# 128-column weights issued as two 64-column halves, with written orders of issue, in a four-layer spectral and state-space kernel

## The chip, the cores and the metric

The kernel runs on one core of a Trainium2 chip. The metric is the device time of one execution in microseconds (us). TensorE is called PE here (its weight loads PEld), VectorE DVE, ScalarE ACT, GpSimd POOL, and SyncE SP.

## What is computed

The input is one sequence of 2048 rows with 512 channels. Four layers follow one another, A, B, A, B, each with a layer norm ahead of it and a residual around it:

```python
def _A_ref(x, w_r, w_i):
    X = rfft2(x, axes=(-2, -1)); X = X * (w_r + 1j * w_i)
    return irfft2(X, s=(S, D), axes=(-2, -1))
def _B_ref(u, log_A_real, A_imag, C_real, C_imag, log_dt, D_skip):
    dt = exp(log_dt); A = -exp(log_A_real) + 1j * A_imag
    C = (C_real + 1j * C_imag) * dt[:, None]
    K = 2.0 * einsum("dn,dnl->dl", C, exp((A * dt[:, None])[:, :, None] * pos)).real
    y = irfft(rfft(u_t, 2 * L) * rfft(K, 2 * L))[:, :, :L]
    return y + u * D_skip
x = A_x
x = x + _A_ref(_layernorm(x), w_r, w_i);  x = x + _B_ref(_layernorm(x), ...)
x = x + _A_ref(_layernorm(x), w_r, w_i);  x = x + _B_ref(_layernorm(x), ...)
```

A is a two-dimensional Fourier transform, a product with fixed weights, and the transform back. B is a convolution along the rows with a kernel K for each of the 512 channels, made from 128 decaying oscillations a channel; both B layers use the same K.

## The kernel before

All transforms are matrix products with constant matrices, in two factors (2048 = 16 x 128 for A, 4096 = 32 x 64 x 2 for B), in f32, which PE does in two passes. Every layer runs in steps, and a step is a Python function that issues a few matmuls and what takes their results out of PSUM.

Layer A (`layer_a`): `spread` (in the second layer A `spread_four`) normalizes the rows and does the first factor along the rows, four products of 128 columns of weights by 128 of data for each of 16 groups (L462, L492). `middle` runs over 16 groups of frequencies: `forward` does the transform along the channels (L503 to L507) and copies it out as `z` on ACT (L517), `weigh` does the second factor in pairs through `side_by_side` (L322) and multiplies by the weights on DVE (L533) and adds on DVE and POOL (L538), `back` returns along the second factor (L551). `end` goes back along the channels (`fold`, L580 to L583) and the rows (`rows_back`, L601).

The convolution kernel K (`kernel_parts`, `kernel_time`): `kernel_parts` prepares phases and logarithms, mostly on DVE, and writes them in three bf16 parts to memory. `kernel_time` then makes K in 32 units of two halves: `grow` (matmul L847, ACT exponential), `bend` (matmuls L857 and L858 in bf16, rounding `kw` on DVE at L860, matmul L861 that subtracts it), `sine` and `cosine` on ACT into a tile `qp` (L826), `terms` on DVE (L879, L881), and `total` (matmul L892, 64 columns of weights, alternating between the two column halves of the array). `kernel_freq` transforms K, 128 channels at a time, and keeps it in memory.

Layer B (`layer_b`): for each of four blocks of 128 channels, `rows` (64*64 tiles: four quarters of the array at once), a transpose of 32x32 squares on DVE (L660), `pair` (64-column weights, `side_by_side`), products with K on DVE (L984), sums on POOL and DVE (L996), `units` (one 128-column product L1004 and 64 small ones of 64 columns, copied out by ACT at L1009), and `rows` again with the residual (L1023).

`side_by_side` at L322 issues products that lie on different parts of the array, so that they run at the same time. Where a product has 128 columns of weights it is one matmul.

The order of work before: the streams of steps are interleaved in Python (`interleave`), and a scheduler then orders the instructions of each engine, with hints at a few places (`issue_after` and a high priority, in `side_by_side`, `ordered`, `spread_four`, `units` and `fetch`). Tiles of a pool take turns in a fixed number of buffers ("rooms"), and which tile gets which follows from the schedule too.

## Time and profile before

| What | Value |
|---|---|
| runs (median, lowest, highest of 3) | 778.15, 777.2, 783.55 us |
| profiled execution, and its span | 785.32 us, 783.6 us |
| mean granted clock of PE | 0.922 |
| PE busy, matmuls | 81%, 7248 |
| DVE busy, instructions | 82%, 1283 |
| ACT busy, instructions | 55%, 928 |
| POOL busy, instructions | 53%, 596 |

How to read the rows: a line such as L462 is a line of the kernel before; `p<-w,w` is the tile that is written and those that are read, without numbers; `128*64` is a matmul's rows and columns of weights, and what follows is the data that it streams. "f32 x96" is a count. The time of a matmul ends when its results are out, so matmuls that follow one another overlap, and the distance of two starts tells what one costs. In the waits, a line names who waited, for whom, how long in all, how often, and the longest.

### The profile page before, as it was taken

How to read it: one execution, taken by the hardware profiler on the slowest of the kernel's cores; microseconds unless marked ns; L12 is line 12 of the kernel's file. 1: busy time of each engine (PE TensorE's matmuls, PEld its weight loads, DVE VectorE, ACT ScalarE, POOL GpSimd, SP SyncE). 2: the span in 40 equal slices, each digit the busy share in tenths (PEclk: the TensorE clock that was granted, in tenths of full speed). 3: DMA queues.
4: the chain of work that ended last, by engine and by line, in shares of the span. 5: the costliest groups of instructions: out<-in, count | busy, mean ns of one | idle time of the engine just before them, and what ended most of it. 6: DMA issues, size and time to landing. Idle time of an engine off the chain costs nothing. (4 is left out here: it accounts for less than half of the span.)

```text
span 783.6 us, 18760 instructions
## 1 busy us (share of the span) xinstructions
PE 631.2 (81%) x7248; PEld 445.6 (57%) x7248; DVE 642.5 (82%) x1283; ACT 431.3 (55%) x928; POOL 414.0 (53%) x596
## 2 busy tenths in 40 slices
PE   3038799898877986897789887874999897889986
PEld 2037576666544544565365647654877664457666
DVE  5998589698988879868997996778588597788993
ACT  3425997875545875787578725223766335233322
POOL 4587766838350454911675573371055473376850
PEclk9995899999967999999999998877999898799999
DMA  8400452324517542361335449122122104124413
GB/s 286 178 0 21 147 180 63 54 83 103 175 49 170 165 87 64 98 171 44 62 110 129 150 73 280 71 95 68 55 81 82 28 16 147 55 83 137 128 38 109
DMA packets 137337, 81.01 MB, mean 103 GB/s; under 512 B 70977, under 2 KB 116929, under 8 KB 136353
## 3 DMA queue, kind: packets, MB, share of 16 engines
q1 hardware_dynamic: 136992, 79.30, 35.8%
q8 instruction: 57, 0.93, 0.5%
q0 software_dynamic: 256, 0.52, 0.4%
q14 instruction: 32, 0.25, 0.1%
HBM read 54.90 MB, written 25.43 MB: 103 GB/s over the span
## 5 line engine op out<-in xcount | busy, mean ns | idle before, releaser
L996 POOL TENSOR_TENSOR u<-wb,wb 64x512 f32<-64x512 f32 x90 | 128.4, 1427 | 90.4 <-DVE wb L984 75.1
L322 PE MATMUL p<-z,mb 128*64 128x512 f32 (+1 forms) x480 | 104.6, 545 | 9.1 <-DVE wb L984 5.9
L892 PE MATMUL pv<-qp 128*64 128x128 f32 x1024 | 79.9, 300 | 11.6 <-DVE qp L881 6.4
L984 DVE TENSOR_TENSOR wb<-p,kk 128x512 f32<-128x512 f32 x128 | 80.8, 675 | 6.4 <-PE p L322 5.2
L892 PEld LDWEIGHTS pv<-qp 128*64 128x64 f32 x1024 | 63.4, 150 | 39.5 <-ACT stage L900 12.8
L654 ACT COPY z<-p 128x512 f32<-128x512 f32 x96 | 51.5, 599 | 57.5 <-PE p L322 44.3
L322 PE MATMUL p<-mb,u 128*64 128x64 f32 x2048 | 73.4, 236 | 11.4 <-DVE u L996 4.2
L322 PEld LDWEIGHTS p<-mb,u 128*64 128x64 f32 x2048 | 71.2, 151 | 19.7 <-issue 11.6
L881 DVE TENSOR_TENSOR qp<-qp,mag 128x1024 f32<-128x1024 f32 x64 | 81.7, 1282 | 0.9
L1108 POOL TENSOR_SCALAR w<-w,norms 128x128 f32<-128x128 f32 x64 | 51.2, 811 | 52.6 <-DMA w<-h 35.4
L879 DVE SCALAR_TENSOR_TENSOR qp<-qp,mag 128x256 f32<-128x256 f32 x128 | 66.5, 536 | 12.6 <-ACT qp L826 12.0
L660 DVE STREAM_TRANSPOSE z<-z 128x512 f32<-128x512 f32 x96 | 58.5, 674 | 20.4 <-ACT z L654 20.4
L462 PE MATMUL p<-w,w 128*128 128x128 f32 x128 | 30.3, 414 | 46.1 <-DVE w L455 35.4
L533 DVE TENSOR_TENSOR w<-wt,p 128x514 f32<-128x514 f32 x64 | 42.5, 686 | 29.5 <-PE p L322 24.1
L538 POOL TENSOR_TENSOR w<-w,w 64x257 f32<-64x257 f32 x48 | 36.6, 762 | 53.5 <-DVE w L533 48.2
L1009 ACT COPY u<-p 128x512 f32<-128x512 f32 x64 | 37.7, 590 | 47.4 <-PE p L322 45.4
L322 PEld LDWEIGHTS p<-z,mb 128*64 128x64 f32 x480 | 35.3, 144 | 39.6 <-issue 20.9
L462 PEld LDWEIGHTS p<-w,w 128*128 128x128 f32 x128 | 26.4, 303 | 49.7 <-issue 31.9
L826 ACT ACTIVATE kf<-pk 128x512 f32<-128x512 f32 x64 | 38.9, 608 | 24.3 <-PE pk L861 23.8
L592 POOL TENSOR_TENSOR wv<-w 128x254 f32<-128x254 f32 x32 | 26.6, 831 | 45.0 <-DVE w L589 33.2
L551 PE MATMUL p<-ca,w 128*128 128x128 f32 x256 | 40.8, 290 | 8.6 <-POOL w L540 3.9
L322 PE MATMUL p<-t,w 64*64 64x128 f32 x1024 | 43.3, 289 | 5.3 <-issue 2.8
(189 smaller groups left out, 1528.2 us busy)
## 6 DMA issues: line engine op xcount, KB each, us to landing
wt<-in_w SPq DMA_DIRECT2D x32, 257.0 KB
kf<-kk SPq DMA_DIRECT2D x32, 256.0 KB
kk<-kf SPq DMA_DIRECT2D x32, 256.0 KB
u<-in_x SPq DMA_DIRECT2D x16, 256.0 KB
hr<-in_x SPq DMA_DIRECT2D x16, 256.0 KB
kt<-stage SPq DMA_DIRECT2D x32, 128.0 KB
h<-hr SPq DMA_DIRECT2D x16, 256.0 KB
w<-kt SPq DMA_DIRECT2D x32, 128.0 KB
```

The source lines that it names most:

```text
L322: last = self.nc.tensor.matmul(out, weights, data, start=not more, stop=True, skip_group_check=True).ins
L462: nc.tensor.matmul(p[:, b], xf[:, b], t, start=True, stop=True)
L533: nc.vector.tensor_mul(m[pl], W, px[:, None, :].to_broadcast([128, 2, 257]))
L551: nc.tensor.matmul(p[:, oe, v], Y[:, v, 128 * oe:128 * oe + 128], st, start=True, stop=True, skip_group_check=True)
L654: nc.scalar.copy(tiles["z"][:, :, :, b, m:m + 2].rearrange("p u j m r -> p (u j) (m r)"), ps[b].rearrange("p u j m r -> p (u j) (m r)"))
L660: nc.vector.transpose(tiles["zt"][:, u:u + 8].rearrange("p u j d -> p (u j d)"), tiles["z"][:, u:u + 8].rearrange("p u j b m r -> p (u j b ...
L879: nc.vector.scalar_tensor_tensor(QP[:, c, 0], QP[:, c, 1, :, ::-1], -1.0 if c else 1.0, m[:, 0], op0=ALU.mult, op1=ALU.mult)
L881: nc.vector.tensor_mul(t, t, mag[:, None, 1:3, 256 * j:256 * j + 256].to_broadcast([128, 2, 2, 256]))
L892: nc.tensor.matmul(p[64 * t:64 * t + 64, g], QP[:, c, 2, d:d + 2].rearrange("p s a -> p (s a)"), QP[:, c, 0:2, d:d + 2].rearrange("p k s b ...
L984: nc.vector.tensor_mul(split(m[c, pl], "du", [32, 16]), by_channel(p), split(k[c], "du", [32, 16]))
L996: self.added = e[0].tensor_sub(y[0:64], v[0, 0], v[1, 1]), e[1].tensor_add(y[64:128], v[0, 1], v[1, 0])
L1108: (self.nc.gpsimd if XNE[k] == "g" else self.nc.vector).tensor_scalar(t[:, k], t[:, k], scale, bias, op0=ALU.mult, op1=ALU.add)
```

## The change

Two things change. First, a helper `halves` issues each matmul with 128 columns of weights as two with 64 columns, to the lower and the upper half of the output's partitions. It replaces every such matmul: L462, L492, L503 to L507, L551, L580 to L583, L601, L847, L857, L858, L861 and L1004. The data streamed is the same, once for each half.

Second, the hints are taken out. A table `TURNS` has for each engine the numbers of its instructions, as the program issues them, in the order in which they shall stand, and `take_turns` ties each to the one before. A table `ROOMS` says which buffer each tile of a pool takes. The tables are lists of numbers, of which a line each is shown.

```diff
+    def room(self, tag):
+        pool, name, tag, size, n = self.tags[tag]
+        if n == 1:
+            return pool, tag, size, n
+        r = self.rooms.setdefault((name, tag), iter(ROOMS[name + "." + tag]))
+        return pool, tag + next(r), size, 1
...
+    def halves(self, out, weights, data, **k):
+        k["skip_group_check"] = True
+        for r in range(2):
+            self.nc.tensor.matmul(out[64 * r:64 * r + 64], weights[:, 64 * r:64 * r + 64], data, **k)
...
         for out, weights, data, *more in products:
-            with ExitStack() as stack:
-                if last is not None:
-                    stack.enter_context(self.tc.issue_after(last))
-                    stack.enter_context(self.tc.high_priority(20000))
-                last = self.nc.tensor.matmul(out, weights, data, start=not more, stop=True, skip_group_check=True).ins
+            last = self.nc.tensor.matmul(out, weights, data, start=not more, stop=True, skip_group_check=True).ins
...
-                nc.tensor.matmul(p[:, b], xf[:, b], t, start=True, stop=True)
+                self.halves(p[:, b], xf[:, b], t, start=True, stop=True)
...
-            nc.tensor.matmul(p, self.ni, whole, start=False, stop=True, skip_group_check=True)
+            self.halves(p, self.ni, whole, start=False, stop=True, skip_group_check=True)
...
+TURNS = {
+    "tensor": """
...
+4520-4535 4508-4519 4536-4537 4544-4559 4538-4543 4560-4567""",
...
+ROOMS = {
...
+    "k.kw": "0101010101101010101010101010101010101010101010101010101010101010",
...
+def take_turns(tc):
+    nc = tc.nc
+    nosync = mybir.DependencyInfo(mybir.DependencyClass.NoSync, mybir.DependencyReason.DATA)
+    work = [i for i in nc.cur_bb.bb.instructions if i.opcode != "TilePoolBoundary"]
+    for name, turns in TURNS.items():
+        own = [i for i in work if i.engine == getattr(nc, name).engine]
+        spans = [[int(k) for k in t.split("-")] for t in turns.split()]
+        order = [own[k] for t in spans for k in range(t[0], t[-1] + 1)]
+        for before, i in zip(order, order[1:]):
+            tc.add_manual_dep(i, before.name, nosync, reason="turns")
...
     with tile.TileContext(nc, schedule_with_timeline_sim=True) as tc:
         net_kernel(tc, **args)
+        take_turns(tc)
```

In the changed kernel `halves` issues at L328 and `side_by_side` at L334, and the lines from L860 on stand a few further down (`kw` at L865, the terms at L884 and L886). The rows below are the order of issue on one engine; the numbers behind a tile's name tell tiles apart, the first of them alike in both kernels, `x2` is a count, and the size is that of the output.

On PE in the first layer A's middle, before: `bend` for two half units (`pk_661`, `pk_677`) stands between the transforms of `forward` (`p_234`), `back` (`p_227`) and the pairs of `weigh` (`p_222`, `p_224`).

```order
L322 MATMUL p_222_952<-w_873,ca_633 64x257 x2
L322 MATMUL p_224_957<-w_873,ca_633 64x257 x2
L551 MATMUL p_227_968<-ca_633,w_893 128x128
L857 LDWEIGHTS th_599
L857 MATMUL pk_677<-kb_86,th_599 128x256
L858 LDWEIGHTS th_599
L858 MATMUL pk_677<-kb_86,th_599 128x256
L861 LDWEIGHTS ni_87
L861 MATMUL pk_661<-kw_660,ni_87 128x512
L503 MATMUL p_234_1009<-ca_633,x_80 128x2x2x33
L505 MATMUL p_234_1009<-ca_633,x_80 128x2x64
```

The same place on PE with the change (the two half units are now `pk_737` and `pk_756`):

```order
L334 MATMUL p_224_1086<-w_991,ca_703 64x257 x2
L328 MATMUL p_227_1097<-ca_703,w_1011 64x128 x2
L328 MATMUL p_234_1145<-ca_703,x_80 64x2x2x33 x2
L328 MATMUL p_234_1145<-ca_703,x_80 64x2x64 x2
L328 LDWEIGHTS ni_87
L328 MATMUL pk_737<-kw_736,ni_87 64x512
L328 LDWEIGHTS ni_87
L328 MATMUL pk_737<-kw_736,ni_87 64x512
L328 MATMUL p_234_1145<-ca_703,x_80 64x128 x4
```

Every output has 64 partitions now, each product stands twice, and the first subtraction (`kw` into `pk`) moved behind two of the four transforms.

On DVE in the first layer A's end, before: rounding (`kw`, L860) and terms (`qp`, L879 and L881) of the units of the third group stand between the sums of `fold` (L588, L589), `rows_back` (L607) and the statistics of the rows.

```order
L607 TENSOR_TENSOR hr_578_2347<-hr_578_2347,p1_579_2349 128x512
L879 SCALAR_TENSOR_TENSOR qp_421_1775<-qp_421_1775,mag_382_1637 128x256
L860 TENSOR_SCALAR kw_428_1804<-pk_429_1805 128x512
L879 SCALAR_TENSOR_TENSOR qp_421_1775<-qp_421_1775,mag_382_1637 128x256
L345 BN_STATS bst_590_2382<-hr_570_2317 128x6
```

The same place on DVE with the change:

```order
L884 SCALAR_TENSOR_TENSOR qp_411_2000<-qp_411_2000,mag_368_1811 128x256
L598 TENSOR_TENSOR w_483_2327<-p1_481_2316,w_482_2325 128x256
L865 TENSOR_SCALAR kw_428_2080<-pk_429_2081 128x512
L617 TENSOR_TENSOR hr_500_2401<-hr_500_2401,p1_501_2403 128x512
L884 SCALAR_TENSOR_TENSOR qp_421_2044<-qp_421_2044,mag_382_1879 128x256
```

The rounding `kw_428` stands behind `hr_578` before and ahead of even `hr_500` with the change, which is several rows of the sequence earlier, and the terms of `qp_421` now begin after it.

On PE in the last layer, before: the small matmuls of `units` (`mb,u`), sixteen for each of the output tiles `p_1749` to `p_1760`, then a pair of the next block (`z,mb`), then the 128-column product L1004.

```order
L322 MATMUL p_1749_8247<-mb_2577,u_7283 64x64 x16
L322 MATMUL p_1750_8265<-mb_2577,u_7283 64x64 x16
L322 MATMUL p_1759_8305<-mb_2577,u_7283 64x64 x16
L322 MATMUL p_1760_8323<-mb_2577,u_7283 64x64 x16
L322 MATMUL p_1768_8390<-z_8381,mb_2577 64x512
L322 MATMUL p_1768_8390<-z_8381,mb_2577 64x32
L322 MATMUL p_1768_8390<-z_8381,mb_2577 64x480
```

The same place on PE with the change:

```order
L334 MATMUL p_1749_9060<-mb_2971,u_8091 64x64 x12
L334 MATMUL p_1750_9078<-mb_2971,u_8091 64x64 x4
L334 MATMUL p_1759_9118<-mb_2971,u_8091 64x64 x2
L334 MATMUL p_1749_9060<-mb_2971,u_8091 64x64 x4
L334 MATMUL p_1759_9118<-mb_2971,u_8091 64x64 x6
L334 MATMUL p_1750_9078<-mb_2971,u_8091 64x64 x2
L334 MATMUL p_1759_9118<-mb_2971,u_8091 64x64 x8
L334 MATMUL p_1750_9078<-mb_2971,u_8091 64x64 x10
L334 MATMUL p_1760_9136<-mb_2971,u_8091 64x64 x10
L328 MATMUL p_1774_9228<-u_8091,mb_2971 64x32 x2
L334 MATMUL p_1760_9136<-mb_2971,u_8091 64x64 x6
```

The sixteen matmuls of a tile no longer stand together: three tiles are mixed, and the product of L1004 (`p_1774`, now two) stands inside the last one's.

## The prediction

> **What bounds the kernel now.** I read the page's busy shares first, then the busy time by stage, then who waits for whom, and last the order of time on TensorE where two shapes of weights alternate. The first fence has the page's heads; the second the stages (busy microseconds of each engine and, in brackets, its instructions).

> ```profile
> span 783.6 us, 18760 instructions
> PE 631.2 (81%) x7248; PEld 445.6 (57%) x7248; DVE 642.5 (82%) x1283; ACT 431.3 (55%) x928; POOL 414.0 (53%) x596
> ```

> ```profile
> 0.00:80.00 80.00, 33.45 (x142) 29.52 (x143) 67.05 (x149) 32.99 (x77) 49.33 (x90) 0.88 0.36 122
> 80.00:240.00 160.00, 138.00 (x1026) 95.14 (x1025) 136.92 (x258) 115.42 (x249) 100.31 (x184) 0.93 0.38 109
> 240.00:440.00 200.00, 170.81 (x2242) 107.00 (x2242) 170.93 (x323) 144.10 (x273) 95.18 (x104) 0.94 0.44 110
> 440.00:540.00 100.00, 75.60 (x1205) 56.19 (x1201) 78.25 (x157) 34.82 (x68) 53.94 (x51) 0.87 0.47 131
> 540.00:640.00 100.00, 90.85 (x615) 72.74 (x616) 73.83 (x185) 52.59 (x165) 42.73 (x103) 0.92 0.17 49
> 640.00:784.00 144.00, 122.50 (x2026) 84.96 (x2024) 115.56 (x216) 51.42 (x99) 72.48 (x65) 0.94 0.33 97
> ```

> No engine is the bound alone. PE and DVE are busy 81% and 82%, and from 80 to 540 us they are level: 384.4 us of PE against 386.1 us of DVE in 460 us. From 540 to 640 PE leads (90.9 against 73.8), from 640 on it leads a little (122.5 against 115.6). Before 80 us PE mostly waits. So the kernel is two nearly equal engines that wait for each other, with ACT between them:

> ```profile
> PE p L462 <- DVE w L455: 35.4, 7, 28.2
> PE pk L861 <- DVE kw L860: 8.9, 13, 2.1
> PE pk L857 <- ACT qp L826: 7.3, 11, 1.8
> PE pv L892 <- DVE qp L881: 6.4, 10, 1.0
> DVE qp L879 <- ACT qp L826: 12.0, 14, 1.7
> ACT u L1009 <- PE p L322: 45.4, 52, 6.0
> ```

> Each row has the total, how often, and the longest. The first lies before 80 us. The next four are the chain that makes the convolution kernel (bend, sine, terms, total): 8.9 + 7.3 + 6.4 + 12.0 = 34.6 us of waiting along it.

> **What a change of tile shape costs.** The next rows are PE's matmuls in order of time: start, length with the pipeline's tail, line, tile shape (rows*columns of weights), count. An f32 product has two passes, hence x2.

> ```profile
> 100.50 0.27 PE L857 MATMUL pk<-kb,th 96*128 96x256 bf16 x1
> 100.61 0.27 PE L858 MATMUL pk<-kb,th 96*128 96x256 bf16 x1
> 100.81 1.09 PE L322 MATMUL p<-w,ca 128*64 128x257 f32 x8
> 101.83 0.49 PE L551 MATMUL p<-ca,w 128*128 128x128 f32 x2
> 102.15 0.28 PE L857 MATMUL pk<-kb,th 96*128 96x256 bf16 x1
> ...
> 103.04 0.39 PE L506 MATMUL p<-ca,x 128*128 128x128 f32 x2
> 103.26 0.39 PE L507 MATMUL p<-ca,x 128*128 128x128 f32 x2
> ...
> 108.78 1.09 PE L892 MATMUL pv<-qp 128*64 128x128 f32 x16
> 109.71 1.04 PE L322 MATMUL p<-w,ca 128*64 128x257 f32 x8
> 110.67 0.39 PE L861 MATMUL pk<-kw,ni 128*128 128x512 bf16 x1
> ```

> Within one shape a full-width pass over 128 columns of data takes 0.11 us (L506 to L507: 0.22 for two), and 256 columns of bf16 take 0.11 (L857 to L858). Where the shape changes, time is lost at four spots. Into the halves: L858 starts at 100.61 and L322 only at 100.81, so 0.09 is lost; the eight passes then last 1.02 (100.81 to 101.83) but 0.96 when the work before them had the same shape (109.71 to 110.67), 0.06 for weights that could not be loaded ahead. Out of them: the eight passes are four on each column half, 4 x 0.22 = 0.88 for 257 columns, against 0.96, so 0.08 of draining; and the first full-width product takes 0.32 (101.83 to 102.15) in place of 0.22, 0.10 more. There and back costs 0.33 us, **0.165 a change of shape**.

> The same rows say what a product in halves costs. L892's sixteen passes are eight on each half: 0.93 us (108.78 to 109.71), less the 0.06 of its own entry, is 0.109 for a pass on both halves at once, the same as one full-width pass. So I cost the split itself at nothing; what hides it is that the two halves stream side by side.

> **The change part by part.**

> *Fewer changes of shape.* Counted in the order of issue, PE changes shape 350 times before and 82 times after (only the 64*64 shape is left beside 128*64): 204 fewer up to the second layer A's spread, 34 fewer in that layer, 30 fewer in the last layer. At 0.165 that is 33.7, 5.6 and 5.0 us of PE's time, 44 in all.

> *More instructions.* 816 products become 1632, of which 256 were bf16 (one pass each) and 560 f32 (two passes): 1376 more passes and as many loads. Such small ones stand in the trace:

> ```profile
> 743.91 3.84 PEld L322 LDWEIGHTS p<-mb,u 128*64 128x64 f32 x128 [0.44 <-issue]
> 743.94 3.95 PE L322 MATMUL p<-mb,u 128*64 128x64 f32 x128 [0.35 <-DVE z L660]
> ```

> 128 passes with their 128 loads need 3.95 us, 0.031 each, so the four passes of a split product could be issued in 0.12 us where the array needs 0.22. Nothing is added while the array has 128 or more columns to stream; the 32-column products at L1004 would need 0.12 in place of the 0.41 they last now, which the changes of shape already count.

> *Loads of bf16 weights.* Before the change these are:

> ```profile
> L892 PEld LDWEIGHTS pv<-qp 128*64 128x64 f32 x1024 | 63.4, 150 | 39.5 <-ACT stage L900 12.8 <-issue 6.8 <-DVE qp L881 4.8
> L551 PEld LDWEIGHTS p<-ca,w 128*128 128x128 f32 x256 | 33.9, 194 | 18.5 <-POOL w L540 7.0 <-DVE w L540 3.9 <-POOL w L539 3.5
> L861 PEld LDWEIGHTS <-ni 128*128 128x128 bf16 x64 | 5.9, 98 | 13.7 <-issue 13.2
> ```

> A 128-column bf16 load takes 98 ns, an f32 one 194 ns, a 64-column f32 one 150 ns. A 64-column bf16 load is not in the trace. It lies between half of 98 ns (no loss) and 150 ns, where the pair costs 300 - 98 = 202 ns more; over 256 products that is 0 to 52 us of loading. I take 0 for the time, since loads run under the pass before (L857 and L858 start 0.11 apart although each has its load), and keep the other end as a rival. [...]

> *What the cut in PE's time is worth.* Before 80 us nothing, PE waits there. From 80 to 540 us DVE needs as much as PE, so between none and all of 33.7 comes through; I take half, 17, since the engines are level. In the second layer A PE leads by 17 us: 5 of 5.6. In the last layer it leads by 7: 4 of 5.0. Late next is DVE in each place. Sum 26.

> *The order from tables.* It keeps the program and moves instructions locally. On DVE the rounding step (L860) stands further ahead of its terms (L879): the median over the 64 half units goes from 10 rows to 12.5, the largest from 35 to 65. That gives the chain PE to ACT to DVE more room, so of its 34.6 us of waits I take a third, 11. The ends are all 34.6 gained, and the loss of the second rival below. SP's and POOL's orders move by a few places (POOL by 20 at most, SP by 18), and neither engine is more than half busy, so I cost them at nothing; if DVE's steps came later, POOL would cover less. ACT loses one load of a table, early, where it is 33 of 80 us busy: nothing. Buffers named in the table are as many as before: nothing.

> Sum: 26 + 11 = 37 us less. The profiled execution took 785.3 us (783.6 of them the span), the median of the three runs is 778.15, a ratio of 0.991. 785.3 - 37 = 748.3, times 0.991 is **741 us**.

> **The rivals.**

> *DVE sets the pace, and the cut is hidden.* For it: whole stretches in which DVE never rests,

> ```profile
> 280.00:300.00 20.00, 15.88 (x119) 6.03 (x117) 19.58 (x31) 12.52 (x23) 11.29 (x11) 1.00 0.38 64
> 300.00:320.00 20.00, 14.12 (x237) 10.91 (x235) 20.00 (x26) 10.99 (x23) 14.17 (x7) 0.91 0.33 95
> 380.00:400.00 20.00, 14.58 (x160) 8.76 (x158) 20.00 (x29) 11.43 (x23) 9.91 (x7) 0.87 0.19 54
> ```

> though PE is idle there for a quarter. Against it: over 80 to 540 us DVE rests 74 of 460 us. Then only layer A's 5 us come through: 780.3, times 0.991, 773 us, no change that can be told.

> *Mixed tiles come late.* The tables mix the small matmuls of up to three output tiles (the order quoted ahead shows it), where before each tile's sixteen stood together. A tile takes a quarter of the 3.95 us above, 0.99. With three mixed, the first is ready 2.0 late, the second 1.0, a mean of 1.0, for 64 tiles whose copies (ACT u L1009) wait for PE already, 45.4 us. If two thirds of these 64 us lie on the path, the time is 785.3 - 26 + 43 = 802, times 0.991, 795 us, slower. It decides for slower from 34 of the 64 tiles on (26 + 8). Against it: the mixed work is in part the pair products that DVE waits for, which come earlier.

> *The bf16 loads set the pace of making the kernel.* If a third of the 52 us shows, 17 us: 748.3 + 17 = 765, times 0.991, 758 us. Against it: PEld is busy 107 of 200 us in that stage.

> *All of it comes through.* The 44 us of changes of shape and 25 of the 34.6 us of waits: 716, times 0.991, 710 us. For it: both engines rest 74 us between 80 and 540.

> **How the numbers follow.** About 1% is what a measurement of this kernel can tell from no change. I give the forecast (725 to 757) a chance of 0.52, all of it 0.15, slow bf16 loads 0.08, DVE setting the pace 0.09, mixed tiles 0.16. The first three are faster: 0.75; the fourth is the same: 0.09; the fifth slower: 0.16. The range must leave out no more than 0.2: it reaches from 706, just under all of it, to 778, over the hidden case, and leaves out the slower case and a few hundredths below.

> **What would show it.** Right: no 128*128 and no 96*128 row in the new profile; L892, z,mb and ca rows follow one another without the 0.09 to 0.10 us steps; PE's busy time falls by 30 to 50 us while DVE's stays near 642; the stage from 80 to 540 shrinks by some 25 us, the second layer A by 5. Wrong: PE's passes on the two halves start one after the other in place of together (a 128-column product over 0.25 us); bf16 loads of 64 columns near 150 ns with waits before L861's successors; waits of ACT u L1009 on PE well over 45 us; or DVE's rests growing although PE is quicker. The forecast fails most easily in the half that I took for 80 to 540 us, and in the third of the chain's waits.

## The result, and the profile after

The changed kernel takes 751.12 us (median of four runs, 750.87 to 756.38), the kernel before 777.67 beside it on the same chip (775.77 to 783.55): a ratio of 0.966, with a 95% interval of 0.960 to 0.973. That is 26.5 us less; 741 were forecast, in a range of 706 to 778. Run again beside later experiments it took 749.84 (ratio 0.965, 0.961 to 0.969).

The head of the page after, to be held against the first fence of the prediction:

```profile
span 754.6 us, 21513 instructions
PE 600.8 (80%) x8624; PEld 452.8 (60%) x8624; DVE 629.5 (83%) x1283; ACT 432.4 (57%) x927; POOL 404.9 (54%) x596
```

PE is busy 30 us less, with 1376 more matmuls; in a second profiled execution of the same kernel it is 593.5, 38 less, so a busy time of PE is good to some 7 us. But DVE, with the same 1283 instructions, is busy 13 us less as well, and it was expected to stay near 642. The stages:

```profile
0.00:80.00 80.00, 30.08 (x260) 22.85 (x262) 67.80 (x150) 32.27 (x74) 48.15 (x90) 0.96 0.38 123
80.00:240.00 160.00, 131.37 (x1568) 96.85 (x1564) 137.01 (x256) 118.92 (x255) 98.77 (x188) 0.96 0.44 122
240.00:440.00 200.00, 171.93 (x2476) 127.63 (x2478) 170.22 (x346) 148.84 (x280) 103.21 (x116) 0.91 0.43 107
440.00:540.00 100.00, 76.35 (x1216) 58.69 (x1214) 80.90 (x183) 35.21 (x85) 40.12 (x35) 0.86 0.46 115
540.00:640.00 100.00, 89.72 (x1168) 69.68 (x1168) 77.99 (x178) 55.40 (x155) 49.35 (x116) 1.00 0.21 60
640.00:755.00 115.00, 101.33 (x1956) 77.12 (x1948) 95.63 (x176) 41.76 (x81) 65.30 (x51) 0.97 0.39 112
```

From 80 to 540 us DVE now leads (388.1 against 379.7 of PE); it was 386.1 against 384.4. The same stretch holds more of the work than before, since everything behind it has moved forward.

The matmuls in order of time, in the stretch of layer A's middle that the prediction priced:

```profile
105.66 0.41 PE L328 MATMUL pk<-kw,ni 128*64 128x512 bf16 x2
106.05 0.44 PE L328 MATMUL p<-ca,w 128*64 128x128 f32 x4
106.32 0.39 PE L328 MATMUL pk<-kb,th 96*64 96x256 bf16 x4
106.54 0.39 PE L328 MATMUL p<-ca,w 128*64 128x128 f32 x4
106.76 0.39 PE L328 MATMUL p<-ca,x 128*64 128x128 f32 x4
106.98 0.39 PE L328 MATMUL p<-ca,w 128*64 128x128 f32 x4
...
109.11 0.39 PE L328 MATMUL pk<-kb,th 96*64 96x256 bf16 x4
109.33 1.04 PE L897 MATMUL pv<-qp 128*64 128x128 f32 x16
110.20 0.39 PE L328 MATMUL p<-ca,w 128*64 128x128 f32 x4
```

From 106.32 to 106.98 each product in halves starts 0.22 after the one ahead of it, as at full width, whatever its kind: the two halves run side by side, and the steps of 0.09 and 0.10 us between shapes are gone. That is what the prediction asked to see.

The waits along the convolution kernel's chain, and ACT's for the small products (total, how often, longest):

```profile
ACT u L1013 <- PE p L334: 49.7, 34, 5.9
...
DVE kw L865 <- PE pk L328: 14.4, 10, 2.7
...
PE pk L328 <- DVE kw L865: 8.1, 12, 2.0
...
PE pv L897 <- DVE qp L886: 6.1, 7, 1.4
PE pk L328 <- ACT qp L833: 6.0, 5, 1.8
```

PE's three waits (8.1, 6.0, 6.1) are hardly shorter than before (8.9, 7.3, 6.4). DVE's wait for the sines, 12.0 before, is 0.9, as the rows of DVE below show. But its rounding `kw` now waits 14.4 us for PE; before it was

```profile
DVE kw L860 <- PE pk L858: 2.4, 3, 1.2
```

So the chain has moved its waiting to another place and kept its amount: 37.0 us in these five rows before, 35.5 now.

DVE's rows tell where its 13 us went. Before (busy, mean ns of one, idle before it):

```profile
L879 DVE SCALAR_TENSOR_TENSOR qp<-qp,mag 128x256 f32<-128x256 f32 x128 | 66.5, 536 | 12.6 <-ACT qp L826 12.0
...
L996 DVE TENSOR_TENSOR u<-wb,wb 64x512 f32<-64x512 f32 x38 | 45.6, 1199 | 0.6
```

And after:

```profile
L884 DVE SCALAR_TENSOR_TENSOR qp<-qp,mag 128x256 f32<-128x256 f32 x128 | 56.7, 468 | 1.1 <-ACT qp L833 0.9
L1001 DVE TENSOR_TENSOR u<-wb,wb 64x512 f32<-64x512 f32 x38 | 35.6, 940 | 0.5
```

The same operations of the same size became shorter by 9.8 and 10.0 us, more than the 13 in all; small differences of other rows go the other way. Neither has a matmul in it. The reason stands in the order of time of DVE and POOL in the kernel before; first DVE:

```profile
300.32 1.20 DVE L881 TENSOR_TENSOR qp<-qp,mag 128x1024 f32<-128x1024 f32 x1
301.45 1.48 DVE L879 SCALAR_TENSOR_TENSOR qp<-qp,mag 128x256 f32<-128x256 f32 x1
302.86 0.67 DVE L860 TENSOR_SCALAR kw<-pk 128x512 bf16<-128x512 f32 x1
303.46 0.41 DVE L879 SCALAR_TENSOR_TENSOR qp<-qp,mag 128x256 f32<-128x256 f32 x1
```

And POOL:

```profile
300.47 2.19 POOL L996 TENSOR_TENSOR u<-wb,wb 64x512 f32<-64x512 f32 x1 [4.82 <-DVE wb L984]
```

The second of these L879 takes 0.41, the first 1.48, and the first lies beside a sum of POOL. That sum took 2.19 where 1.28 is its median. I read it so: it began beside L881, was held up until that ended, and then held up L879 until it ended itself at 302.66. Over the whole trace before, L879 has a median of 0.418 where POOL rests and of 1.22 in the 16 cases beside such a sum; DVE's own sums take 0.67 where POOL rests and 1.37 beside one of POOL's. Both engines have two inputs in SBUF there. In the order from the tables 6 of the L879's meet such a sum in place of 16, and 25 of DVE's sums in place of 28, for shorter times (medians of 0.72 and 0.82 us). Such a meeting is called a collision below. Who began first counts in it: over both traces, the 36 of DVE's sums beside a sum of POOL that had begun ahead of them took a median of 1.40 us, the 17 that had begun first themselves 0.68. Beside POOL's one-input operations it is otherwise, as the last section shows.

### The profile page after: what moved, and what is told of

Its sections match the earlier page's. It is cut to its first block, busy times and chain, and to the rows that moved or that the text cites. A ratio compares the mean times of both kernels' runs of the same rounds, so it can differ in the third digit from the quotient of the medians.

```text
span 754.6 us, 21513 instructions
## 1 busy us (share of the span) xinstructions
PE 600.8 (80%) x8624; PEld 452.8 (60%) x8624; DVE 629.5 (83%) x1283; ACT 432.4 (57%) x927; POOL 404.9 (54%) x596
## 5 line engine op out<-in xcount | busy, mean ns | idle before, releaser
L334 PE MATMUL p<-z,mb 128*64 128x512 f32 (+2 forms) x480 | 106.1, 529 | 4.8 <-DVE wb L989 3.3
L897 PE MATMUL pv<-qp 128*64 128x128 f32 x1024 | 86.4, 299 | 16.2 <-ACT stage L905 9.2
L334 PEld LDWEIGHTS p<-mb,u 128*64 128x64 f32 x2048 | 75.8, 141 | 16.8 <-issue 9.1
L334 PE MATMUL p<-mb,u 128*64 128x64 f32 x2048 | 77.3, 225 | 6.6 <-POOL u L1001 2.6
L886 DVE TENSOR_TENSOR qp<-qp,mag 128x1024 f32<-128x1024 f32 x64 | 80.9, 1266 | 1.8
L1111 POOL TENSOR_SCALAR w<-w,norms 128x128 f32<-128x128 f32 x64 | 48.0, 762 | 51.7 <-DMA w<-h 26.5
L670 DVE STREAM_TRANSPOSE z<-z 128x512 f32<-128x512 f32 x96 | 59.5, 676 | 18.5 <-ACT z L664 18.5
L328 PE MATMUL p<-w,w 128*64 128x128 f32 x256 | 29.9, 403 | 49.4 <-DVE w L467 30.9
L328 PE MATMUL pk<-kb,th 96*64 96x256 bf16 (+1 forms) x384 | 59.9, 327 | 9.8 <-ACT qp L833 6.0
L1013 ACT COPY u<-p 128x512 f32<-128x512 f32 x64 | 36.2, 589 | 50.0 <-PE p L334 49.7
L334 PE MATMUL p<-t,w 64*64 64x128 f32 x1024 | 52.1, 312 | 11.0 <-DMA w<-kt 4.4
L884 DVE SCALAR_TENSOR_TENSOR qp<-qp,mag 128x256 f32<-128x256 f32 x128 | 56.7, 468 | 1.1 <-ACT qp L833 0.9
L334 PEld LDWEIGHTS p<-z,mb 128*64 128x64 f32 x480 | 38.6, 140 | 30.4 <-issue 12.9
L865 DVE TENSOR_SCALAR kw<-pk 128x512 bf16<-128x512 f32 x64 | 43.6, 683 | 15.6 <-PE pk L328 14.4
L328 PEld LDWEIGHTS p<-w,w 128*64 128x64 f32 x256 | 22.6, 205 | 56.4 <-issue 32.8
L334 PEld LDWEIGHTS p<-t,w 64*64 64x64 f32 x1024 | 42.5, 153 | 20.4 <-issue 7.0
## 6 DMA issues: line engine op xcount, KB each, us to landing
kt<-stage SPq DMA_DIRECT2D x32, 128.0 KB
w<-kt SPq DMA_DIRECT2D x32, 128.0 KB
```

What stands on the lines that cost most here:

```text
L328: self.nc.tensor.matmul(out[64 * r:64 * r + 64], weights[:, 64 * r:64 * r + 64], data, **k)
L334: last = self.nc.tensor.matmul(out, weights, data, start=not more, stop=True, skip_group_check=True).ins
L670: nc.vector.transpose(tiles["zt"][:, u:u + 8].rearrange("p u j d -> p (u j d)"), tiles["z"][:, u:u + 8].rearrange("p u j b m r -> p (u j b ...
L865: nc.vector.tensor_scalar(whole, p, MAGIC, -MAGIC, op0=ALU.add, op1=ALU.add)
L884: nc.vector.scalar_tensor_tensor(QP[:, c, 0], QP[:, c, 1, :, ::-1], -1.0 if c else 1.0, m[:, 0], op0=ALU.mult, op1=ALU.mult)
L886: nc.vector.tensor_mul(t, t, mag[:, None, 1:3, 256 * j:256 * j + 256].to_broadcast([128, 2, 2, 256]))
```

## The experiments

Each was timed beside the kernel before, on the same chip; times are medians, and ratios go with their 95% intervals. In the diffs the tables are left out; where a product becomes full-width again, it stands at the place of one of its two halves, and the other's number is dropped from the order.

### The order alone

```diff
     def halves(self, out, weights, data, **k):
-        for r in range(2):
-            self.nc.tensor.matmul(out[64 * r:64 * r + 64], weights[:, 64 * r:64 * r + 64], data, **k)
+        self.nc.tensor.matmul(out, weights, data, **k)
```

> The changed kernel with its tables, but every split product is one full-width matmul again, at the place of its second half. PE changes shape 393 times (82 in the changed kernel, 350 before), 311 more; at 0.165 us that is 51 us of PE's time. If the halves are what helped (26 us for 268 changes of shape), this runs at 751 + 26 x 311/268 = 781 us, no faster than before. If the order of issue alone helped, it stays near 751 us. If both did in the proportion of the forecast (26 to 11), it runs near 772 us.

Measured: 771.14 us against 776.59, ratio 0.992 (0.989 to 0.996). That is the third of the expected times. With the tables, full-width products change shape 393 times, 43 more than before; PE is busy 631.8 us, as before, DVE 633.3, 9 less. So the order alone brings 5 to 7 us.

### The halves alone

```diff
-    "tensor": """ (the order of the change)
+    "tensor": """ (the order of the kernel before, each product's two halves one behind the other)
```

The other engines' orders and the rooms are those of the kernel before too.

> The split products in the order of issue and the buffers of the kernel before: its order is written into the tables, each split product's two halves at the place of the one. PE changes shape 116 times (350 before), 234 fewer, 39 us of PE's time at 0.165. If the halves are what helped, about 751 to 755 us. If the order alone helped, 775 to 778 us. If both did in the proportion 26 to 11, about 759 us.

Measured: 766.38 us, ratio 0.987 (0.982 to 0.992). That is none of the three expected times: it lies between the second and the third. Shapes change 116 times in place of 350; PE is busy 593.1 us, 38.1 less than before, which is 0.163 for each of the 234 changes. Part of that is no price of a change: 5.0 us of it lie before 80 us, where no change of shape was taken away and the granted clock was 0.88 before and 0.98 here.

```profile
0.00:80.00 80.00, 28.47 (x302) 21.69 (x304) 67.36 (x150) 34.47 (x79) 49.37 (x90) 0.98 0.37 122
```

The rest is 0.14 a change. DVE stays at 641.4. But the time falls by only 10 to 11 us, so a good quarter of what PE gained came through.

### One group of products back to full width

```diff
-            self.halves(p[:, 0:129], u[1][0], k["Q"][0], start=False, stop=True, skip_group_check=True)
+            self.halves(p[:, 0:129], u[1][0], k["Q"][0], full=x is not None, start=False, stop=True, skip_group_check=True)
...
-            self.halves(p[:, 384:512], u[0][1], k["Q"][3], start=True, stop=True, skip_group_check=True)
+            self.halves(p[:, 384:512], u[0][1], k["Q"][3], full=x is not None, start=True, stop=True, skip_group_check=True)
```

> The changed kernel, but in the second layer A's fold two of the four products (those at the third and the second line, 32 products in all) are full-width again, which puts 62 changes of shape into a stretch where PE leads, and nothing else is altered. At 0.165 us each this is 10.2 us of PE's time. If a change of shape costs that and PE sets the pace there, 751 + 8 to 10 = 759 to 761 us. If DVE sets the pace and PE's losses are hidden, 751 to 753 us. If a change costs more than the rows of the profile showed (0.3 us, say, with the pipeline's tail), 765 us or more.

Measured: 759.42 us, ratio 0.977 (0.972 to 0.982), 8.3 more than the change, for 62 more changes of shape: 0.13 each, most of the price, as the prediction took it for the second layer A. By the profile 5 of the 8 us lie in that stage (104.0 us against 99.1, from its first matmul to the first of the last layer) and 2 behind it; in a second profile of the change the two stretches are as long as in the first, to 0.1 us.

### The bf16 products back to full width

```diff
-                self.halves(p, th[:, h, slot], c, start=True, stop=True)
+                self.halves(p, th[:, h, slot], c, full=True, start=True, stop=True)
...
-            self.halves(p, self.ni, whole, start=False, stop=True, skip_group_check=True)
+            self.halves(p, self.ni, whole, full=True, start=False, stop=True, skip_group_check=True)
```

And L857 and L858 in the same way.

> The changed kernel with only the bf16 products of the convolution kernel (four kinds, 256 products) at full width again, each at the place of its second half. That puts 261 changes of shape back (82 to 343) and takes 256 loads away. Theory 1, the price of a change of shape: 261 x 0.13 to 0.165 = 34 to 43 us more of PE's time, of which, where PE and DVE are level, four to five tenths come through: 765 to 773 us. Rival, the bf16 loads of 64 columns: two of them take 229 ns where one of 128 columns takes 98, so this kernel has 33.5 us less of loading; if loads set the pace the time falls below 751, to 740 or so. If both count alike it stays near 751.

Measured: 762.08 us, ratio 0.982 (0.977 to 0.987), 12 more than the change beside it (749.84). That is 3 below the 765 to 773 that the price of a change of shape gave, and on the other side of what slow loads gave. The matmuls of this kernel in order of time:

```profile
104.92 0.39 PE L328 MATMUL pk<-kw,ni 128*128 128x512 bf16 x1
105.24 0.44 PE L332 MATMUL p<-ca,w 128*64 128x128 f32 x4
105.61 0.39 PE L328 MATMUL pk<-kb,th 96*128 96x256 bf16 x2
105.94 0.44 PE L332 MATMUL p<-ca,w 128*64 128x128 f32 x4
106.21 0.39 PE L332 MATMUL p<-ca,x 128*64 128x128 f32 x4
```

From 105.24 to 105.94 the pair of products takes 0.70, where the changed kernel takes 0.44 (106.32 to 106.76): 0.13 for each of the two changes of shape. The loads, in the change:

```profile
L328 PEld LDWEIGHTS <-th 96*64 96x64 bf16 x384 | 28.6, 115 | 24.6 <-issue 17.8 <-DMA th<-parts 2.5 <-PE pk L328 0.6
L328 PEld LDWEIGHTS <-ni 128*64 128x64 bf16 x128 | 10.7, 114 | 14.9 <-issue 14.4
```

A load of 64 bf16 columns takes 115 ns, two 229, where one of 128 columns took 98: over 256 products 33.5 us more of loading, inside the bounds of 0 to 52. In PEld's busy time the kernels differ by 19.3 us (428.5 against 447.8), and the one with less loading is slower. So the loads run beside the passes for the most part; that a few us of them show, and make up the 3 us, isn't excluded. PE's busy time rose by 19.5 us only (593.5 to 613.0), 0.075 for each change, less than the rows say; why is open.

### Mixed tiles taken apart

Of each output tile of layer B the small products stand together, at the place of the first of them; PE's order alone is edited, and the changes of shape stay at 82.

```diff
-    "tensor": """ ... 3576-3579 3581 3583 3580 3582 3585 3587 3584 3586 ...
+    "tensor": """ (the numbers of one tile's small products in one run)
```

> The changed kernel, but the sixteen (or eight) small matmuls of each of 96 output tiles in both layers B stand together, at the place of the first of them, as they did in the kernel before; nothing else moves. If mixed tiles come late and this costs on the path, it is faster than 751 us, by 1.0 us for every tile on the path, up to 64 us. If the mixing is neutral, it stays within 3 us of 751. If the mixing was what let the pair products through earlier, it is slower by some us.

Measured: 760.14 us, ratio 0.980 (0.973 to 0.986): 9 us slower than the change, the third of the expected cases. ACT's wait for the small products is 49.5 us there against 49.7, so tiles that stand together are not ready sooner in any way that counts. Its last layer, from the first matmul of its `rows` on, takes 132.6 us against 126.9.

A milder edit sorts the small products by tile only inside stretches that no other product interrupts, so that pair products stay among them.

> The changed kernel, with the small products of the convolution layers' output tiles sorted by tile inside each stretch that no other product interrupts: 615 of 4568 places move, a pair product stays where it was among them, and the changes of shape stay at 82. With each tile's products all together, and so the pair products moved behind them, the time was 760, 9 more. Theory, what the mixing wins is that a pair product, for which DVE waits, comes between the small products: then this kernel stays within 2 of 751. Rival, the mixing of tiles itself wins (the array's halves or the tiles' reads): then it loses several of the 9 us, 755 to 760. If mixing itself costs, as the third rival of the prediction had it, it falls below 749.

Measured: 755.34 us, ratio 0.976 (0.969 to 0.982), with runs from 750.37 to 758.6. That is past the 2 us of the theory and at the lower edge of the rival's 755 to 760, and its interval overlaps those of both neighbours. In its profile the last layer takes 128.3 us, close to the 126.9 of the change, which favours the pair products; it is not settled.

### POOL's sums with one input

The collisions were tested by a change on POOL alone, in three kernels: the change, the halves in the old order, and the kernel before (its order and rooms written as tables). In place of each of its sums POOL multiplies one product by 1, and the other product is left out, so these kernels don't compute the convolution; what they tell is times alone.

```diff
-                self.added = e[0].tensor_sub(y[0:64], v[0, 0], v[1, 1]), e[1].tensor_add(y[64:128], v[0, 1], v[1, 0])
+                self.added = [a.tensor_scalar(o, p[-1], 1.0, None, op0=ALU.mult) if a is eng else f(o, *p) for a, f, o, p in
+                              ((e[0], e[0].tensor_sub, y[0:64], (v[0, 0], v[1, 1])), (e[1], e[1].tensor_add, y[64:128], (v[1, 0], v[0, 1])))]
```

> The changed kernel once more, so that the kernels beside it have it on the same chip: 751 us, within 2 of the first time, a ratio of 0.966.

Measured: 749.84 us, ratio 0.965 (0.961 to 0.969).

> The changed kernel with POOL's 90 sums of products (64x512, two inputs) made into a multiplication by 1 of the input that comes last, so that POOL reads one input there; the other product is left out of the sum. Theory, collisions: an operation of DVE with two inputs in SBUF is held up while POOL works on two inputs. In the changed kernel 6 of the 128 rounding-free products of the convolution kernel (128x256) and 25 of DVE's own 38 sums lie beside such a sum of POOL and take 2.7 and 9.7 us more than undisturbed. These 12 us of DVE's busy time go, the 38 sums come down from a mean of 940 to about 690 ns, and the time falls by 3 to 10 us, to 741 to 748. [...] Rival, the tables work by slack for PE's chain alone: DVE's rows keep their length and the time stays at 751, or falls by a microsecond or two since POOL is quicker.

Measured: 754.77 us, ratio 0.970 (0.966 to 0.975). The time rose by 5 us, so this expectation failed. Its rows for DVE and for POOL:

```profile
L1001 DVE TENSOR_TENSOR u<-wb,wb 64x512 f32<-64x512 f32 x38 | 26.1, 690 | 0.5
```

```profile
L1001 POOL TENSOR_SCALAR u<-wb 64x512 f32<-64x512 f32 x90 | 140.2, 1559 | 62.6 <-DVE wb L989 56.5
```

DVE's sums did come down to 690 ns, as an undisturbed one takes (0.67 us before, 0.69 in the change), and DVE's busy time fell by 12.5 us (631.0 to 618.5). But the one-input form is slower on POOL itself, 1.49 us by its median where the sum took 1.28, and now it is POOL that is held up (a mean of 1.56). DVE waits 14.9 us for buffers that POOL empties, in place of 4.9. My reading, which no run tests by itself, is that in the order from the tables this costs more than the collisions left there.

> The halves in the order of the kernel before, with POOL's sums of products made one-input in the same way (one product left out of each). Theory, collisions: in this order 16 of the 128x256 products and 28 of DVE's sums lie beside such a sum of POOL and take 12.6 and 15.4 us more than undisturbed, 28 us against 12 in the order from the tables. So DVE's busy time falls by some 28 from 641, and the time by 10 to 20 from 766, to 746 to 756: most of the distance between the two orders closes. Rival, slack for PE's chain: both orders fall by the same few microseconds, and the distance of some 15 us between them stays.

Measured: 752.82 us, ratio 0.969 (0.964 to 0.973), 13.6 less than the halves alone. DVE is busy 613.7 us, 27.7 less, as expected, and both rows came down (66.9 and 43.0 us in the halves alone):

```profile
L884 DVE SCALAR_TENSOR_TENSOR qp<-qp,mag 128x256 f32<-128x256 f32 x128 | 56.0, 452 | 13.6 <-ACT qp L833 13.2
L1001 DVE TENSOR_TENSOR u<-wb,wb 64x512 f32<-64x512 f32 x38 | 29.0, 763 | 0.6
```

So the old order gains some 14 us without the collisions, although the one-input form is slower on POOL. The buffer of the product that is left out can go sooner too, but little can come of that: DVE's waits for buffers that POOL empties were 1.6 us in the halves alone and are 1.4 here. The old order is now 2 us ahead of the order from the tables, where it was 15 behind. That does not make the collisions the distance between the two orders: by the table below, the tables still win 5.5 us in the last layer (129.7 against 135.3), and the old order comes 7.5 us earlier to it (617.2 against 624.7). The two cancel.

> The kernel before, all products at full width and every instruction in its old order, with POOL's sums of products made one-input (one product left out of each). In the halves in the old order this took 13.6 us (766.4 to 752.8). Here 16 products of 128x256 and 28 of DVE's sums are held up, by 11.4 and 18.1 us, 29.5 of DVE's busy time, while PE stays at 631. Theory, two level engines: the gain on one comes through only as far as the other falls too, so without the halves less of it shows than with them: 4 to 9 us, to 768 to 773. Rival, the two gains simply add: 13 to 14 us, to 763 or 764. If nothing changes, the collisions cost nothing as long as PE has its changes of shape.

Measured: 760.15 us, ratio 0.980 (0.974 to 0.986), 17 us less than before (16 by the ratio), and DVE busy 617.4 in place of 642.5. My theory that two level engines hide each other's gains fell: the rival, that the two gains add, was nearer, and even more came than its 13 to 14. So the collisions cost that much without any halves. PE's busy time was expected to stay at 631 and is 619.0; against the 589.7 of the same kernel in halves that is 0.125 for each of the 234 changes of shape.

### Where each gain lies

The starts are those of the first matmul of the second layer A and of the last layer's `rows`, in the order of time of each profiled execution; the last column sums, over DVE's operations with two inputs in SBUF (L879, L881, L996, and the 64x257 sums at L538 and L539, of the kernel before), what each took above the median of the undisturbed in the kernel before, before and behind the first of these starts. Executions of one kernel differ by up to 7 us up to the first start (the change: 528.6 and 521.5), so that column is read with care.

| Kernel | second A starts | last layer starts | span | from there on | DVE held up |
|---|---|---|---|---|---|
| before | 543.0 | 645.1 | 783.6 | 138.5 | 31.8 + 16.0 |
| halves alone | 532.9 | 630.5 | 767.1 | 136.6 | 33.1 + 12.5 |
| order alone | 533.5 | 637.7 | 765.7 | 128.0 | 18.1 + 11.4 |
| the change | 528.6 | 627.7 | 754.6 | 126.9 | 16.7 + 10.4 |
| the change again | 521.5 | 620.5 | 747.5 | 127.0 | 17.7 + 11.5 |
| mixed tiles apart | 527.3 | 626.4 | 759.0 | 132.6 | 18.9 + 10.4 |
| halves, one-input sums | 520.7 | 617.2 | 752.5 | 135.3 | 13.8 + 5.3 |
| the change, one-input sums | 525.7 | 624.7 | 754.5 | 129.7 | 11.6 + 5.8 |
| before, one-input sums | 520.9 | 621.9 | 757.6 | 135.6 | 15.7 + 6.2 |

The tables take about half of DVE's delays away up to the second layer A (33.1 to 16.7 with the halves, 31.8 to 18.1 without). In the last layer they win some 10 us, whether the products are split (136.6 to 126.9) or not (138.5 to 128.0). These 10 are not the collisions: with one-input sums the old order still takes 135.3 there, although DVE's delays behind the first start fell from 12.5 to 5.3. Nearly 6 of the 10 are lost again when the mixed tiles are taken apart (132.6); the other 4 were not traced. So of the 15 us between the halves in the old order and the change some 10 lie in the last layer and 5 ahead of it, where the collisions are. That the collisions are what makes those 5 is likely, but not shown: no run changes them alone within the order from the tables without slowing POOL.

The second layer A (from the first start to the second) takes 102.1 us before, 97.6 with the halves alone, 104.2 with the order alone and 99.1 with the change: the halves shorten it by 5 in either order, and the tables lengthen it by 2. The head became 3 us longer too: the last matmul of the first layer's spread starts at 79.0 in place of 76.0.

## Why the prediction came out as it did

The time lay inside the range and on the right side, 10 us above the forecast: 26.5 of the 37 us came. How they split depends on which part is taken first. Halves first, they bring 10 and the tables then 15; tables first, they bring 5 to 7 and the halves then 20. The forecast was 26 and 11. So the first term was too large either way, and the second is near in one way of counting by luck, since its mechanism was another.

- *The price of a change of shape* (0.165 us) was right to about a quarter: 0.14 of PE's busy time in the halves alone without the head, 0.125 between the two kernels with one-input sums in the old order, 0.13 of time in the second layer A, 0.13 in the rows of the bf16 experiment. Only PE's busy time in the bf16 experiment says less, 0.075.
- *Splitting costs nothing*, *more instructions cost nothing*, *the bf16 loads are hidden*: right as far as the rows go (0.22 us from one f32 product in halves to the next, as at full width), up to a few us for the loads. A load of 64 columns takes 115 ns against 98 for 128, yet the kernel that takes them back is slower (762.08 against 749.84 us), not faster, and none of the waits shown is for a load.
- *What the cut in PE's time is worth* (17 + 5 + 4): this is the step that failed. It gave 26 us for 268 changes of shape; at that rate the 234 in the old order make 23 and the 311 in the order from the tables 30, and 10 and 20 came. By stage, with the profiled executions, the second layer A gave the 5 forecast in either order (102.1 to 97.6 and 104.2 to 99.1), the last layer 1 to 2 in place of 4, and the part ahead of the second layer A 5 to 12 in place of 17, where executions of one kernel differ by up to 7. "Half, since the engines are level" had no row under it: level busy times over 460 us do not say which engine ends a wait in each piece.
- *The order from tables* (11 us from the chain's waits): 15.3 us between the halves in the old order and the change (766.4 to 751.1), 5 to 7 without the halves, and the mechanism wrong. Of the 34.6 us of waits, DVE's 12.0 went, but 12.0 came back at `kw` (2.4 to 14.4). What the runs show in its place is 10 us in the last layer, of which the mixing there holds nearly 6, and half as much delay of DVE by POOL ahead of it. POOL's order was put at nothing because it moves "by a few places" and POOL is not "more than half busy". It is busy 53%, and what counted was not its share but what stands beside what (an L879 takes 0.418 us where POOL rests and 1.22 beside one of its sums).
- *Mixed tiles come late*, the slower rival, was the opposite of the truth: taking them apart, which also puts the pair products behind them, costs 9 us.
- *DVE's busy time stays near 642* was wrong, and it is what gave the mechanism away: the same 1283 instructions were busy 642.5 us before and 629.5 after, so something had stretched them.

What stays open: whether the mixing in the last layer wins by the pair products between the small ones, what the other 4 us there are, and why the halves seem worth 20 us in the order from the tables (771.1 to 751.1) and 10 to 11 in the old order. Part of that may be that the tables give full-width products 43 more changes of shape, 7 us of PE's time at 0.165; the rest wasn't tried. Nor were the buffers of `ROOMS` tried apart from the orders, or the kernel before with its own order written as tables.

## What to carry to other kernels

Compare the longest and the median duration of each group of equal instructions on DVE: where the mean is well above the median (536 against 418 ns here), look at what POOL does at those moments, for some 16 us lay there in the kernel before that no wait list shows. What relief on one of two equally busy engines is worth can't be taken from their shares: the same halves gave 10 us in one order and 20 in the other. And when two changes come together, run each alone, since their sum can come out near with a term wrong.

## What the runs showed of the hardware

```profile
311.74 1.22 DVE L886 TENSOR_TENSOR qp<-qp,mag 128x1024 f32<-128x1024 f32 x1
312.88 0.75 DVE L884 SCALAR_TENSOR_TENSOR qp<-qp,mag 128x256 f32<-128x256 f32 x2
313.67 1.22 DVE L886 TENSOR_TENSOR qp<-qp,mag 128x1024 f32<-128x1024 f32 x1
314.81 1.51 DVE L884 SCALAR_TENSOR_TENSOR qp<-qp,mag 128x256 f32<-128x256 f32 x4
```

```profile
312.29 6.44 POOL L1111 TENSOR_SCALAR w<-w,norms 128x128 f32<-128x128 f32 x4 [4.32 <-DMA w<-h]
```

The four took 6.44 us, and none of DVE's operations shown beside them is longer than it is alone (1.22 us for an L886, 0.42 for an L884). Of the 29 L884's that lie longest beside such a scaling in the changed kernel none takes over 0.6 us, though in 20 of these cases the scaling had started first; beside a sum with two inputs it is 3 of 6, and 14 of 16 in the kernel before, up to 1.50. Beside the one-input sums (64x512) of the three test kernels it is 11 of 59, none above 0.84. So the form on POOL's side has a part in who waits, besides who came first (1.40 against 0.68 us for DVE's sums, as above).
